# Six K and V loads of a two-layer decode kernel, each issued as 96 rows and four times 8 rows

## The chip, the cores and the metric

One core of one Trainium2 chip runs the whole kernel. The metric is the device time of one execution in microseconds (us), and the time before is the median of three runs. All operands are bf16 in device memory; the engines compute out of an on-chip memory of 128 partitions, and 16 DMA engines bring the data there.

## What is computed

Four sequences are at one new token each (B = 4, Sq = 1, D = 512). Block A is grouped-query attention over a cache: 32 query heads share 8 K and V heads, 4,096 cached positions, head width 128. Block B is a gated feed-forward of width F = 1,792. The two blocks are applied twice, with the same weights and the same caches:

```python
def _A_ref(x, k_cache, v_cache, wq, wo):
    q = (x @ wq).reshape(B, Sq, 32, 128).transpose(0, 2, 1, 3)
    k = jnp.repeat(k_cache, 4, axis=1)          # (4, 8, 4096, 128) -> 32 heads
    v = jnp.repeat(v_cache, 4, axis=1)
    scores = jnp.einsum("bhqd,bhkd->bhqk", q, k) * (128 ** -0.5)
    o = jnp.einsum("bhqk,bhkd->bhqd", softmax(scores), v)
    return o.transpose(0, 2, 1, 3).reshape(B, Sq, 4096) @ wo

def _B_ref(x, w_gate, w_up, w_down):
    return (sigmoid(x @ w_gate) * (x @ w_up)) @ w_down

x = x + _A_ref(_layernorm(x), ...)
x = x + _B_ref(_layernorm(x), ...)
x = x + _A_ref(_layernorm(x), ...)
x = x + _B_ref(_layernorm(x), ...)
```

One K head of one sequence is 4,096 x 128 bf16, that is 1 MB, and so is one V head. There are 32 of each.

## The kernel before

**Units.** A unit is one K head and one V head of one sequence in one layer: 2 x 4 x 8 = 64 units. `ORDER` lists them by hand in pairs, the second layer interleaved with the first as soon as a sequence has its input. For a pair the kernel transposes K (DVE, L1164), takes the scores (PE, L1180), reduces the maximum (DVE, PE L1199 and L1240), takes the exponential (ACT, L1265), turns the probabilities (PE L1310, ACT L1344) and multiplies them with V (PE, L1414). Query projection, the output projection with `wo`, the norms and block B stand between the units, at places that more tables at the head of the file fix by hand.

**Slots.** The on-chip memory has 12 slots of 128 partitions x 8 KB, each for one K or V head (`slot`); the four slices of `wq` become slots 12 to 15 once the queries of the second layer are done. A K head lies in its slot as `(p j) d -> p (j d)`: partition p holds 32 consecutive positions, 8 KB that are contiguous in device memory. V lies the same way, except that V of a pair with `SHARE` above 5 (`by_quarters`, L545) and the last two V come in quarters of 2 KB per partition (the last two V as four transfers each, `v_parts`, L517). `RET` says which heads stay in their slots from the first layer to the second and aren't loaded again.

**Loads.** The strings `LOADS` give the order in which everything is loaded: k, v, o (a piece of `wo`, L528) and s (a piece of the feed-forward weights, L528). The letters k and v count through the units in their order, so ("k", 9) is K of unit 9; units whose head is resident are skipped. `pump()` is called between the steps of the computation and issues, all on SP (SyncE), the next loads in this order as long as a slot is free in the plan; the transfer itself then waits on its semaphore until the last reader of that slot is done. SP issues nothing else but the first loads (L563, L566) and the output (L2084).

**Semaphores.** `_Sched` records all instructions by engine. `group` appends a list of instructions; the first of them gets the waits that follow from what is read and written, and the token of the last is what later readers wait for. `dma` is a group of one transfer that adds 16 to the semaphore of its slot when it has landed (`d0` to `d11`, `wq0` to `wq3`). `prune` and `assign_values` then drop waits that others imply and turn tokens into counts. So a reader of a slot waits until the slot's semaphore has reached a number.

Each load of a K or V head is one transfer of 128 rows, which the last statement of `pump()` issues (L550 in the profile).

Of the kernel before, what the change touches and what calls it, by code (L numbers as in the profile page):

```python
# [169 lines left out]
    71, 124, 3, 38, 71, 44, 6, 4,  # L170
    10,
)


class _Token:
# [135 lines left out]
def bass_interleave_layers__gqa_block_cached__glu_gated_glu__decode_kernel(  # L311
# [17 lines left out]
    P = 128  # L329
# [13 lines left out]
    NSLOT = 12  # L343
# [8 lines left out]
    S = _Sched()  # L352
# [144 lines left out]
    def slot_keys(s):  # L497
        return [f"s{s}"] + ([f"wq{s - NSLOT}"] if s >= NSLOT else [])

    def take():  # L500
        return free.pop(0)

    def by_quarters(n):
        return n < NU - 2 and SHARE[n // 2] > 5
# [5 lines left out]
    def v_parts(s, n):  # L510
        _, b, u = seq[n]
        rows = A_v_cache[b, u].rearrange("(a p j) d -> a p (j d)", a=4, p=P)
        for a in range(4):
            dst = slot[s][:, a * JG * DH:(a + 1) * JG * DH]
            S.dma(
                "sp",
                (lambda dst, src: lambda e: e.dma_start(dst, src))(dst, rows[a]),  # L517
                f"wo{4 * (n % 2) + a}",
                writes=[f"v{n % 2}_{a}"] + (slot_keys(s) if a == 0 else []),
            )  # L520

    def pump():
        while loads:
            kind, n = loads[-1]
            if kind in wparts:
                loads.pop()
                dst, src = wparts[kind](n)
                S.dma("sp", (lambda dst, src: lambda e: e.dma_start(dst, src))(dst, src), f"wo{n}" if kind == "wo" else kind, writes=[f"{kind}{n}"])  # L528
                continue
            if not free:  # L530
                return
            loads.pop()
            s = take()
            _, b, u = seq[n]
            if kind == "k":
                where["kn", n] = s
                src = A_k_cache[b, u].rearrange("(p j) d -> p (j d)", p=P)
            else:
                where["v", b, u] = s
                if n >= NU - 2:  # L540
                    v_parts(s, n)
                    continue
                src = A_v_cache[b, u].rearrange("(p j) d -> p (j d)", p=P)
            dst = slot[s][:, :]
            if kind == "v" and by_quarters(n):  # L545
                dst = dst.rearrange("p (a m) -> p a m", a=4)
                src = A_v_cache[b, u].rearrange("(a p j) d -> p a (j d)", a=4, p=P)
            S.dma(
                "sp",
                (lambda dst, src: lambda e: e.dma_start(dst, src))(dst, src),  # L550
                f"d{s}" if s < NSLOT else f"wq{s - NSLOT}",
                writes=slot_keys(s),
            )

# [6 lines left out]
    for k in range(KD):  # L561
        if k == 1:
# [5 lines left out]
            writes=[f"wq{k}"],  # L568
        )
    pump()  # L570

    dve(lambda e: e.memset(ones_f, 1.0), writes=["ones_f"])
# [18 lines left out]
    fns = []  # L591
# [882 lines left out]
    def o_turn(g):  # L1474
        p = g % 2
        many = 2 - PV_WIDE[g]
        s = stage.pop()
        o_raw = slot[s].bitcast(dt.float32)[:, 0:2 * P * many]
        act(lambda e: e.activation(o_raw, O_ps[p][:, 0:2 * P * many], ACTF.Copy), reads=[f"O{p}"], writes=slot_keys(s))
        fns = []  # L1480
        for n in range(2 * many):
            r = n * REP
            fns.append(
                (lambda n, r: lambda e: e.matmul(
                    O_ps[p][:, 0:2 * OW].rearrange("p (t w) -> p t w", t=2)[:, :, 0:REP],
                    lhsT=o_raw[:, n * P:(n + 1) * P],
                    rhs=o_sel[:, :, r:r + REP],
                    start=(n == 0),
                    stop=(n == 2 * many - 1),
                ))(n, r)  # L1490
            )
        S.group("pe", fns, reads=slot_keys(s) + ["o_sel"], writes=[f"O{p}"])
        free.append(s)
        pump()
# [113 lines left out]
    for m in wo_steps.pop((-1, 0), ()):  # L1608
        wo_turn(m, (M_ps, S_ps)[m % 2], "MS"[m % 2])
    k_turn(0)  # L1610
    pump()
    k_turn(1)
    pump()
# [17 lines left out]
    for b in range(Bn):  # L1631
        n = vstep[last[0, b]] - 1
# [499 lines left out]
```

## Time and profile before

| | |
|---|---|
| Runs | 303.77, 302.91, 303.86 us, median 303.77 |
| Span of the profiled execution | 306.1 us (no time of its own beside it; 0.8% above the median) |
| Granted TensorE clock, mean | 0.88 |
| Instructions | 11,460, of which PE 4,993, DVE 600, ACT 521, POOL 107 |
| Moved | 117.40 MB in 20,094 packets, 384 GB/s over the span |
| Last stretch without loads | from about 292 us to the end |

The profile's page gives first the busy time of each engine, then the span in 40 equal slices (7.65 us each) as tenths, then the DMA queues, the chain of work that ended last, the costliest groups of instructions, and the DMA issues with the median time from issue to landing. A row of the timeline or the chain begins with its start and its length in us. "SPq L550" is SP's issue of a load at line 550; "slot<-in_A_k_cache_dram" is the transfer of a K head into a slot. In a row of stretches the numbers in brackets are instruction counts, and behind them stand the granted clock, the DMA share and the rate in GB/s. In a row of waits the three numbers are the time waited in all, how often, and the longest.

### The profile page before, as it was taken

Reading aid. Unit: us, or ns where it says so; the run is one execution under the profiler, and the core shown is the slowest. Engines: PE = TensorE matmul, PEld = TensorE weight load, DVE = VectorE, ACT = ScalarE, POOL = GpSimd, SP = SyncE. Lnnn points to the kernel's source line nnn. Section 1 sums busy time; section 2 is a strip of 40 time slices with the busy share of each in tenths; the row PEclk is TensorE's granted clock in tenths of the full one; section 3 lists DMA queues with packets and bytes.
Section 4 is the critical chain, followed back from the end, with each engine's and each line's share of the span. In section 5 each row is a group of like instructions: output and inputs, shape, how many; then the busy total and the mean of one; then the engine's idle time right before and its main releaser. Section 6 shows DMA issues by size and latency. Waiting matters only on the chain.

```text
span 306.1 us, 11460 instructions
## 1 busy us (share of the span) xinstructions
PE 224.3 (73%) x4993; PEld 157.6 (51%) x4993; DVE 205.7 (67%) x600; ACT 131.2 (43%) x521; POOL 26.0 (9%) x107
## 2 busy tenths in 40 slices
PE   0384386864687888688886777888868688987886
PEld 0331043543464466566554554665546456556676
DVE  4755677885766368875854997566788668357743
ACT  1031243552205246564451874627772443646310
POOL 0000000000000010000001110001000000012200
PEclk9999999999579897979999857589788979599977
DMA  7999999999999979999999999999999999999900
GB/s 283 420 397 415 422 414 416 418 418 421 418 416 403 388 295 418 423 415 416 388 394 378 415 422 421 419 418 422 420 416 418 413 412 415 400 345 411 377 18 3
DMA packets 20094, 117.40 MB, mean 384 GB/s; under 512 B 1992, under 2 KB 1996, under 8 KB 7500
## 3 DMA queue, kind: packets, MB, share of 16 engines
q1 hardware_dynamic: 20044, 116.67, 93.9%
q8 instruction: 39, 0.64, 0.8%
q14 instruction: 11, 0.09, 0.1%
HBM read 116.66 MB, written 0.00 MB: 381 GB/s over the span
## 4 chain that ended last, share of the span: by engine, by line
DMA 45%; PE 30%; DVE 12%; SPq 5%; ACT 4%; issue 3%; POOL 0%; POOLq 0%; DVEq 0%; ACTq 0%
DMA slot<-in_A_v_cache_dram 22%; DMA slot<-in_A_k_cache_dram 12%; PE O_ps L1414 9%; DMA wd<-in_B_w_down_dram 6%; DVE slot L1164 6%; DMA wo<-in_A_wo_dram 5%; PE S_ps L1180 5%; ACT pT L1344 2%; SPq L550 2%; SPq L528 2%; PE M_ps L636 2%; PE O_ps L1566 2%; PE M_ps L1034 1%; PE M_ps L1087 1%; DVE wo L651 1%
## 5 line engine op out<-in xcount | busy, mean ns | idle before, releaser
L1164 DVE STREAM_TRANSPOSE slot<-slot 128x1024 f32<-128x1024 f32 (+1 forms) x61 | 100.9, 1663 | 7.0 <-DMA slot<-in_A_k_cache_dram 6.9
L1344 ACT ACTIVATE pT<-PT 32x64 bf16<-32x64 f32 x392 | 84.3, 215 | 31.9 <-PE PT L1310 26.9
L1414 PE MATMUL O_ps<-pT,slot 128*128 128x32 bf16 (+2 forms) x1888 | 65.8, 190 | 16.2 <-DMA slot<-in_A_v_cache_dram 9.6
L1414 PEld LDWEIGHTS O_ps<-pT,slot 128*128 128x128 bf16 x1888 | 59.6, 101 | 23.3 <-DMA slot<-in_A_v_cache_dram 10.6
L1180 PE MATMUL S_ps<-slot,qz 128*32 128x256 bf16 x1008 | 48.9, 329 | 12.5 <-DVE slot L1164 7.2
L1265 ACT ACTIVATE pe<-S_ps,small 128x256 bf16<-128x256 f32 x32 | 15.2, 474 | 63.3 <-DVE small L1253 63.2
L1180 PEld LDWEIGHTS S_ps<-slot,qz 128*32 128x32 bf16 x1008 | 25.3, 107 | 24.8 <-DVE slot L1164 9.2
L1279 POOL TENSOR_TENSOR small<-small 128x1 f32<-128x1 f32 x64 | 12.4, 193 | 217.6 <-ACT pe L1265 215.1
L646 ACT ACTIVATE wo<-M_ps 128x512 bf16<-128x512 f32 x14 | 8.3, 595 | 35.0 <-PE M_ps L636 35.0
L1338 DVE CAST pT<-PT 32x64 bf16<-32x64 f32 x88 | 19.4, 221 | 5.6 <-PE PT L1310 4.1
L1566 PE MATMUL O_ps<-oT,wo 128*128 128x32 bf16 x576 | 19.7, 188 | 1.1 <-issue 0.5
L636 PE MATMUL M_ps<-wo,row 64*128 64x512 bf16 x56 | 13.3, 565 | 9.1 <-DVE wo L651 5.5
L1566 PEld LDWEIGHTS O_ps<-oT,wo 128*128 128x128 bf16 x576 | 18.2, 101 | 2.1 <-DVE oT L1505 1.1
L1217 DVE TENSOR_REDUCE small<-S_ps 128x1 f32<-128x256 f32 x32 | 13.2, 413 | 8.0 <-PE S_ps L1180 7.8
L903 POOL TENSOR_TENSOR qz<-qc,norm 128x128 bf16<-128x128 bf16 x32 | 12.6, 399 | 45.5 <-ACT qc L889 45.5
L1240 PE MATMUL MS<-row_max,mask_f 128*128 128x16 bf16 x64 | 6.6, 176 | 13.1 <-DVE row_max L1223 12.6
L651 DVE CAST wo<-M_ps 128x512 bf16<-128x512 f32 x14 | 9.5, 680 | 9.6 <-PE M_ps L636 9.5
L1505 DVE TENSOR_TENSOR oT<-O_ps,rden 128x8 bf16<-128x8 f32 x31 | 4.9, 159 | 14.4 <-PE O_ps L1414 9.8
L1240 PEld LDWEIGHTS MS<-row_max,mask_f 128*128 128x128 bf16 x64 | 4.3, 107 | 19.2 <-DVE row_max L1223 17.7
L1199 PE MATMUL MS<-ident_bf 128*128 128x256 bf16 x69 | 12.2, 316 | 0.4
L1310 PE MATMUL PT<-ident_bf,pe 128*128 128x128 bf16 x64 | 10.0, 245 | 2.9 <-ACT pe L1265 2.6
L1253 DVE CUSTOM_DVE_ANT_0 row_max<-MS,small 128x16 bf16<-128x16 f32 x32 | 7.0, 217 | 7.3 <-PE MS L1240 7.1
(143 smaller groups left out, 231.1 us busy)
## 6 DMA issues: line engine op xcount, KB each, us to landing
slot<-in_A_v_cache_dram SPq DMA_DIRECT2D x49, 1024.0 KB, 12.5
slot<-in_A_k_cache_dram SPq DMA_DIRECT2D x43, 1024.0 KB, 11.3
wq<-in_A_wq_dram SPq DMA_DIRECT2D x4, 1024.0 KB, 7.8
wo<-in_A_wo_dram SPq DMA_DIRECT2D x8, 512.0 KB, 15.8
wq<-in_A_v_cache_dram SPq DMA_DIRECT2D x3, 1024.0 KB, 12.3
slot<-in_A_v_cache_dram SPq DMA_DIRECT2D x8, 256.0 KB, 13.6
wg<-in_B_w_gate_dram SPq DMA_DIRECT2D x2, 896.0 KB, 18.9
wu<-in_B_w_up_dram SPq DMA_DIRECT2D x2, 896.0 KB, 16.2
```

The lines of the kernel that those rows point to most:

```text
L636: (lambda h, i, rows: lambda e: e.matmul(ps[h][:, :], lhsT=spread_w[i][rows, :], rhs=wo_sb[rows, c + i, :], start=(i == 0), stop=(i == 1), ...
L651: lambda e: e.tensor_copy(wo_sb[:, c + 1, :], ps[1][:, :]),
L903: lambda e: e.tensor_tensor(qz_sb[z][:, :, 0:4 * REP].rearrange("p i (a r) -> p i a r", r=REP), qc_sb[:, b, u:u + 2, :, :].rearrange("p u ...
L1164: dve(lambda e: e.transpose(kf, kf), writes=[f"s{st}"])
L1180: (lambda t, b2, e_, w0, s: lambda e: e.matmul(S_ps[p][32 * s:32 * s + 8 * REP, 0:2 * P], lhsT=qzf[:, w0:w0 + 8 * REP], rhs=ktv[:, :, s, : ...
L1217: lambda e: e.tensor_reduce(m, S_ps[p][:, 0:2 * P], AX.X, ALU.max),
L1265: lambda e: e.activation(to, frm, ACTF.Exp, bias=nm_sb[p], scale=exp_scale, accum_out=sm_sb[p][0],),
L1279: (lambda n: lambda e: e.tensor_tensor(sm_sb[p][n + 1], sm_sb[p][n], top(sm_sb[p][n]), ALU.subtract))(n),
L1338: (lambda dst, frm: lambda e: e.tensor_copy(dst, frm))(dst, frm),
L1344: (lambda dst, frm: lambda e: e.activation(dst, frm, ACTF.Copy))(dst, frm),
L1414: (lambda x, c, j: lambda e: e.matmul(O_ps[p][:, ul * OW:ul * OW + PV_WIDE[g]].rearrange("p (w n) -> p w n", n=REP), lhsT=vv[:, x * JG + c ...
L1566: (lambda c, r: lambda e: e.matmul(wide_out(O_ps[p], OWO + c, nb), lhsT=wo_sb[:, u * REP + r, bass.ds(2 * P * (c // 2) + c % 2, P, step=2) ...
```

## The change

Two tables are new, and the last statement of `pump()` builds a group of one transfer per slice of partitions in place of one transfer:

```diff
+EIGHTS = (slice(0, 96), slice(96, 128, 4), slice(97, 128, 4), slice(98, 128, 4), slice(99, 128, 4))
+
+PARTS = {
+    ("k", 9): EIGHTS, ("k", 18): EIGHTS, ("v", 23): EIGHTS,
+    ("k", 40): EIGHTS, ("k", 49): EIGHTS, ("v", 52): EIGHTS,
+}
...
-            S.dma(
+            fns = []
+            for rows in PARTS.get((kind, n), (slice(0, P),)):
+                fns.append((lambda dst, src: lambda e: e.dma_start(dst, src))(dst[rows], src[rows]))
+            S.group(
                 "sp",
-                (lambda dst, src: lambda e: e.dma_start(dst, src))(dst, src),
-                f"d{s}" if s < NSLOT else f"wq{s - NSLOT}",
+                fns,
+                sem_key=f"d{s}" if s < NSLOT else f"wq{s - NSLOT}",
+                inc=16,
+                needed=True,
                 writes=slot_keys(s),
             )
```

For six of the loads the first transfer has the partitions 0 to 95 and each of the four others has eight of the partitions 96 to 127, four apart: 96, 100, ..., 124, then 97, 101, ..., 125, and so on. Each of the five adds 16 to the slot's semaphore, 80 in all, and a reader of the slot waits for all of them. All other loads, their order, and the instructions of all other engines are as before. The lines below the tables move down by 8, and L550 becomes L558.

The six loads go, in the profiled execution before, to slot 5 (issued near 45.6 us), slot 12 (108.3 us), slot 9 (143.0 us), slot 12 (183.1 us), slot 5 (219.3 us) and slot 2 (251.5 us).

## The prediction on record

> **What bounds the kernel now.** I read the page from the top: the DMA lines first, then the chain, then the stretches of time.
>
> ```profile
> span 306.1 us, 11460 instructions
> ...
> DMA  7999999999999979999999999999999999999900
> GB/s 283 420 397 415 422 414 416 418 418 421 418 416 403 388 295 418 423 415 416 388 394 378 415 422 421 419 418 422 420 416 418 413 412 415 400 345 411 377 18 3
> DMA packets 20094, 117.40 MB, mean 384 GB/s; under 512 B 1992, under 2 KB 1996, under 8 KB 7500
> ...
> q1 hardware_dynamic: 20044, 116.67, 93.9%
> q8 instruction: 39, 0.64, 0.8%
> q14 instruction: 11, 0.09, 0.1%
> ...
> DMA 45%; PE 30%; DVE 12%; SPq 5%; ACT 4%; issue 3%; POOL 0%; POOLq 0%; DVEq 0%; ACTq 0%
> ```
>
> The 16 DMA engines are busy for nine tenths or more in all but two of the first 38 slices, and 45% of the chain that ended last is DMA. So this is a kernel that streams, with short places where the stream breaks. Those places are seen in the stretches (columns: window, its length, five engines' busy time, granted clock, DMA share, GB/s):
>
> ```profile
> 60.00:104.00 44.00, 31.20 (x630) 21.63 (x626) 28.77 (x81) 15.05 (x58) 2.25 (x10) 0.84 1.01 414
> 104.00:112.00 8.00, 6.56 (x166) 4.06 (x167) 4.99 (x22) 2.58 (x10) 0.76 (x2) 1.00 0.80 297
> ...
> 120.00:147.00 27.00, 21.61 (x485) 16.15 (x482) 18.77 (x48) 14.61 (x66) 2.21 (x9) 0.90 1.01 418
> 147.00:156.00 9.00, 7.35 (x189) 5.42 (x186) 6.32 (x26) 5.12 (x19) 0.48 (x3) 1.00 0.99 373
> ...
> 176.00:248.00 72.00, 55.95 (x1322) 41.03 (x1318) 52.42 (x139) 38.99 (x165) 6.95 (x29) 0.78 1.01 418
> ...
> 268.00:277.00 9.00, 7.69 (x206) 5.53 (x206) 5.45 (x23) 4.64 (x20) 1.49 (x5) 0.94 0.99 353
> ```
>
> Three long stretches run at 414 to 418 GB/s with every engine full. At 104 to 112, 147 to 156 and 268 to 277 us the rate falls to 297, 373 and 353: there some engines have nothing queued. The chain, in order of time (start, length, piece), says which loads the end hangs on:
>
> ```profile
> 60.33 14.42 DMA slot<-in_A_k_cache_dram
> ...
> 79.90 18.77 DMA wd<-in_B_w_down_dram
> ...
> 112.88 11.82 DMA slot<-in_A_v_cache_dram
> ...
> 125.92 13.82 DMA slot<-in_A_v_cache_dram
> ...
> 142.97 6.67 DMA slot<-in_A_v_cache_dram
> ...
> 207.72 10.57 DMA slot<-in_A_v_cache_dram
> ...
> 219.34 13.83 DMA slot<-in_A_k_cache_dram
> ...
> 239.34 8.69 DMA slot<-in_A_k_cache_dram
> 248.05 1.85 DVE slot L1164
> ```
>
> The last transfer on it lands at 239.34 + 8.69 = 248.03 us. After that the chain is compute and issue alone, down to the end.
>
> **What one load is.** Issues by kind (count, size, median us from issue to landing):
>
> ```profile
> slot<-in_A_v_cache_dram SPq DMA_DIRECT2D x49, 1024.0 KB, 12.5
> slot<-in_A_k_cache_dram SPq DMA_DIRECT2D x43, 1024.0 KB, 11.3
> wq<-in_A_wq_dram SPq DMA_DIRECT2D x4, 1024.0 KB, 7.8
> ...
> wq<-in_A_v_cache_dram SPq DMA_DIRECT2D x3, 1024.0 KB, 12.3
> ...
> wq<-in_A_k_cache_dram SPq DMA_DIRECT2D x1, 1024.0 KB, 7.8
> ```
>
> Packets of 8 KB or more: 20,094 − 7,500 = 12,594. The 1 MB loads of K, V and wq are 49 + 43 + 4 + 3 + 1 = 100; two V loads go by quarters (2 KB pieces), and 98 × 128 rows = 12,544, plus the 50 packets of the two instruction queues, is 12,594 exactly. So a row is one packet. One costs its engine 0.939 × 16 × 306.1 us / 116.67 MB × 8,192 B = 0.323 us. A whole load is 8 packets per engine, 2.58 us; the stream's 418 GB/s gives 2.5. Landing comes 11 to 12.5 us after issue, so four to five loads stand in the queues.
>
> **The change, part by part.** It moves the same bytes in the same rows: packets stay 20,094 and no engine besides SP gets an instruction more. SP gets six times four more issues. The six loads in its issue order (start, us, count in the row):
>
> ```profile
> 44.65 1.36 SPq L550 DMA_DIRECT2D slot<-in_A_k_cache_dram  x2
> ...
> 108.25 4.16 SPq L550 DMA_DIRECT2D slot<-in_A_k_cache_dram  x4
> ...
> 142.97 8.91 SPq L550 DMA_DIRECT2D slot<-in_A_v_cache_dram  x5
> ...
> 183.07 0.33 SPq L550 DMA_DIRECT2D slot<-in_A_k_cache_dram  x1
> ...
> 219.34 0.33 SPq L550 DMA_DIRECT2D slot<-in_A_k_cache_dram  x1
> ...
> 248.88 14.02 SPq L550 DMA_DIRECT2D slot<-in_A_v_cache_dram  x6
> ```
>
> They are the second of the first row, the first of the second and third, the fourth and fifth, and the second of the sixth. Two of them, at 142.97 and 219.34, are themselves pieces of the chain.
>
> *Issues on SP.* One costs 0.33 us, four 1.3 us per split. Nothing new waits: only the 96-row transfer carries the slot's wait. Queued behind it on SP are the next loads, and behind those, compute. What hides it is that SP itself waits for slots most of the time:
>
> ```profile
> SPq L550 <- PE O_ps L1414: 69.0, 26, 4.4
> SPq L550 <- PE S_ps L1180: 55.4, 25, 5.8
> ```
>
> Alone these two are 124 us. With 10 us of transfers queued, 1.3 us more on SP starves nothing, except perhaps at 108.25, where engines are dry and three loads wait behind: 0 to 1.3 us there. I take 0, since the 96 rows give every engine 1.9 us of work before the next load is needed. Without that cover all six would cost 7.8 us.
>
> *Completion.* Readers now wait for five transfers. The last is issued 1.3 us after the first and queues for some 10 us; I cost this at nothing, up to 0.3 us in the load that took only 6.67 us.
>
> *Work per engine.* This is the term that counts. The 96 rows are 6 packets on each engine if they are dealt as evenly as the 128. A transfer of 8 rows is 8 packets, so half the engines get none of it. No row of before shows a transfer of that shape. Bounds: if four such transfers are dealt in turn over all 16 engines, each engine has 8 packets as before, cost 0. If all four go to the same eight, those have 6 + 4 = 10 (3.23 us) and the others 6 (1.94 us), that is 0.65 us above and 0.65 us below the whole load. I take the second end: transfers of one shape, issued one after the other, have no visible reason to be dealt differently. A load has landed when its slowest engine is done, and in a full stream the slow eight stay 0.65 us behind until the queues run dry. So a split costs 0.65 us if the engines were even before.
>
> The sum by stage. The load at 45 us is ahead of the transfers at 60.33 and 79.90, in the stretch at full rate: 0.65. That at 108.25 comes at the end of the first break, ahead of 112.88 and 125.92, and the one at 142.97 is itself on the chain: 1.3. Those of 183.07 and 219.34 lie in the third full stretch, ahead of 207.72, 219.34 and 239.34: 1.3. The sixth, after 248.88, has no transfer of the chain behind it and a break at 268 to absorb it: 0; if the later loads became bound, 0.65. In sum 5 × 0.65 = 3.2 us. I make it against the profiled execution (span 306.1 us) and add it to the median of the runs, 303.77; the profiled one is 0.8% longer, which changes 3.2 by 0.03. Forecast: **307.0 us**.
>
> [...]
>
> **The rivals.**
>
> *Faster: the engines are uneven now, and the change evens them.* The instruction queue's 39 fetches take 0.8% × 16 × 306.1 = 39 us, 1.0 us each. If they all land on the same eight engines, these lose 4.9 us each over the run, the others nothing, and the stream goes at the pace of the eight. If the eight that the small transfers spare are exactly those, six splits give them 6 × 1.29 = 7.7 us relative to the others, against 4.9: the lag is taken away, and then somewhat overdone. The gain is half the lag that builds up in a stretch without a break: 4.9/306 = 0.016 us per us, in stretches of about 44, 35 and 72 us 0.7 + 0.56 + 1.15 = 2.4, half 1.2 us: 302.6. If a fetch costs its engine half as much again, 302.0. For it: any unevenness is invisible in a share of 1.01 averaged over 16 engines. Against it: no grouped row says where the fetches land, and if they fall on the eight that get more, the forecast grows by the same 1.2 us. It decides as soon as the fetched-on eight lag by more than 0.65 us when a split comes.
>
> *Much slower: the two eights get in each other's way at the memory.* The small transfers write partitions 96 to 127. [...] If two engines that share a way into those partitions run at half pace for four packets, that is 1.29 us more on each; the heavy eight then need 3.23 + 1.29 = 4.52 us instead of 2.58, 1.94 us more per split, five of them 9.7 us: 313.5. At half that overlap, 308.6. For it: 418 GB/s is the flat top of the rate line, so something is full; against it: nothing in the rows says whether it is the engines or the way into memory.
>
> [...]
>
> *Nothing: the small transfers are dealt over all engines, or the queues absorb the lag.* 303.8 us. For it: DMA is only 45% of the chain.
>
> **How the numbers follow.** Forecast case (0.9 to 5 us slower) 0.36; much slower 0.20; faster 0.32; nothing 0.12. A measurement of this kernel can tell about 0.3%, 0.9 us. Of the faster case 0.27 is beyond that and 0.05 within; of the last case 0.02 on either side. So faster 0.29, same 0.13, slower 0.58. Range 302.0 to 312.0: from the faster case with the dearer fetch to the much slower one nearly whole, leaving out some 0.08 below and 0.09 above.
>
> **What would show it.** Right: loads issued behind a split land later by about 0.65 us; the chain's pieces at 60.33, 112.88, 207.72 and 239.34 grow; the rate in the full stretches falls from 418 for some us behind each split and the breaks are filled by the light eight. The fast rival: those pieces shrink, and the full stretches hold their rate while the breaks get deeper and earlier. The much slower one: the rate falls clearly in slices with a split, below 400. The issue term is wrong if SP's waits for slots shrink and DMA share falls right behind a split. The forecast is wrong if the even deal before the change, on which 0.65 rests, isn't so.

## The result and the profile after

The changed kernel takes 331.72 us (median of four runs, 329.24 to 336.21), the kernel before beside it 303.81. The ratio is 1.089, 95% interval 1.082 to 1.097. Ratios here and below leave out the few runs that fell into a slower state of the chip, such as the one of 336.21 us. By the ratio that is 27 us more, 4.5 us for each of the six loads, over eight times the rise that was forecast, and above the range's upper end of 312.0. The execution profiled after has a span of 331.4 us.

The page of the changed kernel, the lines that answer to those of before:

```profile
span 331.4 us, 11484 instructions
...
DMA  7999999999999599999989999999999999999930
GB/s 296 416 404 416 422 410 418 280 341 418 421 404 411 196 287 418 419 420 317 265 306 381 414 423 358 276 421 420 420 346 229 402 389 388 254 419 395 407 136 4
DMA packets 20286, 117.40 MB, mean 354 GB/s; under 512 B 2184, under 2 KB 2188, under 8 KB 7692
...
q1 hardware_dynamic: 20236, 116.67, 94.2%
...
DMA 44%; PE 32%; DVE 10%; SPq 6%; issue 3%; ACT 3%; POOL 1%; POOLq 0%; DVEq 0%; ACTq 0%
```

Read the second and third line together. The rate falls to 280, 287, 265, 276, 229 and 254 GB/s in slices 8, 15, 20, 26, 31 and 35, one for each split, and in all six the DMA engines are shown nine tenths busy. So they are not starved: their packets take longer, 0.557 us in the stretch below where the mean of before is 0.323. The slice with 196 GB/s is another case: its digit is 5, and it is the break that the kernel before has too. Share times span of q1 gives the time that an engine spends on packets: 0.939 × 306.1 = 287.4 us before, 0.942 × 331.4 = 312.2 us after, for the same 116.67 MB. That is 24.8 us more per engine, against 25.3 us more span. The loss is nearly all time in which packets are under way.

The stretches around the splits, first the kernel before and then the changed one (window, length, five engines' busy time, granted clock, DMA share, GB/s):

```profile
60.00:70.00 10.00, 6.44 (x160) 4.28 (x153) 8.88 (x21) 5.93 (x24) 0.74 (x3) 1.00 1.01 420
```

```profile
60.00:70.00 10.00, 6.26 (x110) 3.94 (x111) 6.40 (x18) 4.19 (x16) 0.31 (x2) 0.59 1.02 240
70.00:104.00 34.00, 23.81 (x451) 16.32 (x448) 21.60 (x58) 9.63 (x39) 1.54 (x7) 0.70 1.02 414
...
152.00:164.00 12.00, 5.10 (x84) 3.22 (x84) 6.95 (x21) 2.01 (x7) 0.39 (x2) 0.72 1.02 264
...
274.00:286.00 12.00, 8.19 (x180) 5.71 (x179) 8.43 (x24) 4.93 (x18) 0.39 (x2) 0.90 1.03 323
```

From 60 to 70 us, when the first split load passes through the engines, all of them are busy (1.02) and they move 240 GB/s in place of 420. An 8 KB packet then takes 1.02 × 16 × 10 us / 2.4 MB × 8,192 B = 0.557 us, where 0.323 is the mean of before. Right behind it, from 70 us, the rate is back at 414. This loses (420 − 240)/420 × 10 = 4.3 us at one split. The 2.4 MB that pass in these 10 us are as much as 18 packets of 8 KB per engine, and the split load has 8 of them, if its rows are shared out evenly. So packets of the loads around it are slow as well.

Who waits for it stands in the rows of waits of the changed kernel (time in all, times, longest):

```profile
PE O_ps L1427 <- DMA slot<-in_A_v_cache_dram: 23.4, 14, 5.7
...
DVE slot L1177 <- DMA slot<-in_A_k_cache_dram: 19.3, 11, 6.4
```

and in those of the kernel before:

```profile
PE O_ps L1414 <- DMA slot<-in_A_v_cache_dram: 9.6, 12, 1.9
...
DVE slot L1164 <- DMA slot<-in_A_k_cache_dram: 6.9, 7, 1.9
```

PE waits 13.8 us longer for V and DVE 12.4 us longer for K, 26.2 us together (the two can overlap). The chain of the changed kernel has the pieces that the forecast named, longer:

```profile
59.63 19.57 DMA slot<-in_A_k_cache_dram
...
237.98 0.66 SPq L558
238.68 0.62 SPq L558
239.34 0.62 SPq L558
240.01 17.44 DMA slot<-in_A_k_cache_dram
...
272.96 11.25 DMA slot<-in_A_v_cache_dram
```

The K load of 60.33 took 14.42 us before and takes 19.57 now. The piece at 240.01 is the last small transfer of the fifth split, with three issues of that split ahead of it on the chain; the whole load, at 219.34 before, took 13.83 us. The last piece is new: a V load issued ahead of the sixth split now ends a wait after 248 us.

### The profile page after: what moved, and what is told of

The parts are those of the page before. It is cut to its first block, busy times and chain, and to the rows that moved or that the text cites. A ratio compares the mean times of both kernels' runs of the same rounds, so it can differ in the third digit from the quotient of the medians.

```text
span 331.4 us, 11484 instructions
## 1 busy us (share of the span) xinstructions
PE 230.9 (70%) x4993; PEld 161.8 (49%) x4993; DVE 206.6 (62%) x600; ACT 130.9 (39%) x521; POOL 26.0 (8%) x107
## 2 busy tenths in 40 slices
DMA packets 20286, 117.40 MB, mean 354 GB/s; under 512 B 2184, under 2 KB 2188, under 8 KB 7692
## 3 DMA queue, kind: packets, MB, share of 16 engines
q1 hardware_dynamic: 20236, 116.67, 94.2%
## 4 chain that ended last, share of the span: by engine, by line
DMA 44%; PE 32%; DVE 10%; SPq 6%; issue 3%; ACT 3%; POOL 1%; POOLq 0%; DVEq 0%; ACTq 0%
DMA slot<-in_A_v_cache_dram 23%; DMA slot<-in_A_k_cache_dram 11%; PE O_ps L1427 10%; DMA wd<-in_B_w_down_dram 6%; PE S_ps L1193 5%; DVE slot L1177 5%; DMA wo<-in_A_wo_dram 5%; SPq L558 3%; PE M_ps L1047 3%; PE O_ps L1579 2%; SPq L536 2%; ACT pT L1357 1%; PE M_ps L649 1%; PE M_ps L1100 1%; DVE pT L1351 1%
## 5 line engine op out<-in xcount | busy, mean ns | idle before, releaser
L1427 PE MATMUL O_ps<-pT,slot 128*128 128x32 bf16 (+2 forms) x1888 | 68.9, 194 | 29.2 <-DMA slot<-in_A_v_cache_dram 23.4
L1427 PEld LDWEIGHTS O_ps<-pT,slot 128*128 128x128 bf16 x1888 | 62.9, 103 | 35.9 <-DMA slot<-in_A_v_cache_dram 22.6
L1193 PE MATMUL S_ps<-slot,qz 128*32 128x256 bf16 x1008 | 50.6, 340 | 17.3 <-DVE slot L1177 9.2
L1292 POOL TENSOR_TENSOR small<-small 128x1 f32<-128x1 f32 x64 | 12.4, 193 | 244.4 <-ACT pe L1278 241.9
L1518 DVE TENSOR_TENSOR oT<-O_ps,rden 128x8 bf16<-128x8 f32 x31 | 5.0, 160 | 24.8 <-PE O_ps L1427 21.5
L1253 PE MATMUL MS<-row_max,mask_f 128*128 128x16 bf16 x64 | 6.6, 176 | 13.8 <-DVE row_max L1236 13.0
L1047 PE MATMUL M_ps<-wq,xc_bf 128*1 128x512 bf16 x128 | 11.6, 463 | 0.7 <-DVE xc_bf L778 0.5
## 6 DMA issues: line engine op xcount, KB each, us to landing
slot<-in_A_v_cache_dram SPq DMA_DIRECT2D x47, 1024.0 KB, 13.8
```

Of the source, the lines that this page charges most:

```text
L1047: (lambda k, st: lambda e: e.matmul(M_ps[h][32 * st:32 * st + 1, :], lhsT=xc_bf[:, k, 0:1], rhs=wv[:, k, h, :, st, :], start=(k == 0), sto ...
L1193: (lambda t, b2, e_, w0, s: lambda e: e.matmul(S_ps[p][32 * s:32 * s + 8 * REP, 0:2 * P], lhsT=qzf[:, w0:w0 + 8 * REP], rhs=ktv[:, :, s, : ...
L1427: (lambda x, c, j: lambda e: e.matmul(O_ps[p][:, ul * OW:ul * OW + PV_WIDE[g]].rearrange("p (w n) -> p w n", n=REP), lhsT=vv[:, x * JG + c ...
```

## The experiments

Theory P, a guess from the slow packets above (0.557 us where 0.323 was the mean): engines that write at the same time into the same partitions slow each other, so packets take twice as long. The rivals are N, the number of transfers and their issue; U, the uneven share of rows per engine, which was the forecast's term; S, that any transfer below 128 rows is slow; and R, that the place is where rows are read. All experiments change only the tuple `EIGHTS` for the same six loads, except where said. Ratios are to the kernel before on the same chip, with 95% intervals.

**1. Five transfers of 128 rows each.**

```diff
-EIGHTS = (slice(0, 96), slice(96, 128, 4), slice(97, 128, 4), slice(98, 128, 4), slice(99, 128, 4))
+EIGHTS = tuple((slice(0, 128), slice(a, b)) for a, b in ((0, 1024), (1024, 2048), (2048, 3072), (3072, 3584), (3584, 4096)))
```

> Same six loads, each as five transfers on one semaphore, but every transfer has all 128 rows and a part of the columns (three of 2 KB a row, two of 1 KB). Theory P (engines that write into the same partitions halve each other's pace): no change to the partitions, so within 1.5 us of 303.8. Rival N (the number of transfers or their issue costs, 28 us for 24 more): 320 to 332. Rival U (only the uneven share of the engines, as forecast): 303.8.

Measured: 307.80 us, 1.011 (1.003 to 1.018). As many transfers on the same semaphore as in the change cost 3 us, not 27. N falls as the main cause. The 3 us are above what P expected. Part of them is seen on the chain, where the issues of two splits stand for 1.4 us each (144.19 to 145.62 and 218.75 to 220.17 us); experiment 14 returns to the rest.

**2. 96 rows and 32 rows.**

```diff
+EIGHTS = (slice(0, 96), slice(96, 128))
```

> Each of the six loads as 96 rows and one transfer of 32 rows (two per engine). P: the 96 rows and the 32 rows are both slowed, about 1.9 and 0.6 us per split: 314 to 320. N: a quarter of the transfers added, a quarter of the loss: 311. U: every engine has 8 rows again: 303.8.

Measured: 327.23 us, 1.075 (1.067 to 1.082). Here each engine has 6 + 2 = 8 rows again, if they are dealt evenly, and one transfer is added in place of four. More than four fifths of the loss remain, 23 of 27 us. U and N both fall; the value is above the 314 to 320 that I had given P, whose sizes I had underestimated.

**3. The 96 rows alone.**

```diff
+EIGHTS = (slice(0, 96),)
```

> Leaves out rows 96 to 127 of the six loads (stale data there), so 1.5 MB less is moved, worth 3.9 us by the packets. P: the 96 rows alone take nearly twice their 1.9 us: 306 to 311. N and U: nothing is split and the engines are even, so 300.

Measured: 321.47 us, 1.058 (1.053 to 1.063). The kernel moves 1.5 MB less and takes 17.6 us longer, 2.9 us for each of the six. So a loss of this size, two thirds of the whole, needs no small transfer at all: the transfer of 96 rows brings it. P had the sign, but under half the size.

**4. The small transfers alone.**

```diff
+EIGHTS = (slice(96, 128, 4), slice(97, 128, 4), slice(98, 128, 4), slice(99, 128, 4))
```

> Leaves out rows 0 to 95 of the six loads and keeps the four transfers of 8 rows, so 4.5 MB less is moved, worth 11.6 us. P: half the engines spend four rows at half pace or worse and slow the other half meanwhile, 2.5 to 3.5 us in place of 2.58 for a whole load: 303 to 309. N: four transfers cost most of the 4.7 us per split: 310 to 320. U: 1.3 us in place of 2.58 on the busier engines: 296 to 298.

Measured: 309.68 us, 1.021 (1.014 to 1.027). A quarter of the data of these loads takes 6.3 us longer than all of it. So the small transfers cost something as well. Parts 3 and 4 are not to be added: each leaves data out, and how much of its packets' worth that saves is not measured.

**5. The split turned over.**

```diff
+EIGHTS = (slice(32, 128), slice(0, 32, 4), slice(1, 32, 4), slice(2, 32, 4), slice(3, 32, 4))
```

> The same split turned over: rows 32 to 127 in one transfer, rows 0 to 31 in four of eight rows, four apart. [...] If only the second half of the memory were slow for the small transfers, or if the number of transfers counted, 328 to 332 or as the change. [...]

Measured: 327.22 us, 1.074 (1.067 to 1.081). The small transfers now write partitions 0 to 31. Most of the loss remains, 23 of 27 us, so it does not hang on the upper partitions.

**6. Two halves of 64 rows.**

```diff
+EIGHTS = (slice(0, 64), slice(64, 128))
```

> Each of the six loads as two transfers of 64 rows, 0 to 63 and 64 to 127. Same count of transfers as 96 and 32 rows, every engine again has 8 rows. [...] A theory S, by which a transfer of fewer than 128 rows is slow whatever its rows: as 96 and 32 rows, 327. U: 304.

Measured: 330.23 us, 1.087 (1.081 to 1.093). One transfer more per load, none of it small, and every engine even if the rows are dealt evenly: it costs as much as the whole change. This fits S. Whether it fits P hangs on which engines write which partitions, and no row shows that.

**7 and 8. Four transfers of 32 rows: every fourth row, and neighbouring rows.** These two differ in nothing but the rows that each transfer takes.

```diff
+EIGHTS = tuple(slice(i, 128, 4) for i in range(4))
```

> Each of the six loads as four transfers of 32 rows, every fourth row from 0, 1, 2 and 3, so that each transfer reaches all parts of the memory. [...] S: as the four transfers of neighbouring rows. U: 304.

```diff
+EIGHTS = tuple(slice(32 * i, 32 * i + 32) for i in range(4))
```

> Each of the six loads as four transfers of 32 neighbouring rows. [...] S: the same as with every fourth row. U: 304.

Measured: 307.86 us, 1.012 (1.004 to 1.019), with every fourth row; 331.59 us, 1.092 (1.083 to 1.100), with neighbouring rows. S falls: the same size and number of transfers costs 4 us or 28. Page and stretch of the strided kernel:

```profile
span 304.1 us, 11478 instructions
...
DMA packets 20382, 117.40 MB, mean 386 GB/s; under 512 B 2280, under 2 KB 2284, under 8 KB 7788
...
q1 hardware_dynamic: 20332, 116.67, 94.3%
```

```profile
60.00:70.00 10.00, 6.72 (x144) 4.87 (x145) 8.56 (x20) 4.56 (x18) 0.74 (x3) 0.83 1.02 420
```

and of the one with neighbouring rows:

```profile
span 328.1 us, 11478 instructions
...
q1 hardware_dynamic: 20332, 116.67, 94.9%
```

```profile
60.00:70.00 10.00, 4.43 (x86) 2.81 (x87) 6.07 (x17) 3.58 (x14) 0.00 (x0) 0.80 1.02 251
```

With every fourth row an engine spends 0.943 × 304.1 = 286.8 us on packets, as in the kernel before (287.4); with neighbouring rows 0.949 × 328.1 = 311.4. At 60 to 70 us the rates are 420 and 251 GB/s, at the same DMA share of 1.02.

The count of packets under 512 B goes with the rows of the transfers. It rises from 1,992 to 2,184 with the change, by 8 for each of its 24 small transfers, and the 96 rows leave the count of their load as it was (1,992 in experiment 3); with 18 added transfers of 32 rows it rises to 2,280, by 16 each. Read as one small packet from each engine that has a part of the transfer, this would be 8 engines for 8 rows and 16 for 32; that reading is my estimate from the counts, and which engines they are no row shows.

**9 and 10. Reading and writing taken apart.** `PARTS` gives a pair here, the partitions written and the rows read:

```diff
-            for rows in PARTS.get((kind, n), (slice(0, P),)):
-                fns.append((lambda dst, src: lambda e: e.dma_start(dst, src))(dst[rows], src[rows]))
+            for to, of in PARTS.get((kind, n), ((slice(0, P), slice(0, P)),)):
+                fns.append((lambda dst, src: lambda e: e.dma_start(dst, src))(dst[to], src[of]))
```

```diff
+EIGHTS = tuple((slice(i, 128, 4), slice(32 * i, 32 * i + 32)) for i in range(4))    # 9
+EIGHTS = tuple((slice(32 * i, 32 * i + 32), slice(i, 128, 4)) for i in range(4))    # 10
```

> Each of the six loads as four transfers of 32 rows that are read from neighbouring rows of the cache and written to every fourth partition. This changes the computation: the rows of these six heads lie in other partitions than their counterparts. If the loss comes from where the rows are written (P): as the four strided transfers, 306 to 309. If it comes from where they are read (R): as the four neighbouring ones, 330.

> The counterpart: read from every fourth row of the cache, written to 32 neighbouring partitions; the rows of these six heads again lie elsewhere. P: 329 to 333. R: 306 to 309.

Measured: written to every fourth partition 307.99 us, 1.014 (1.010 to 1.019); written to neighbouring ones 331.44 us, 1.091 (1.087 to 1.094). The time follows the partitions written and not the rows of the cache that are read. The stretch of the two kernels, 9 and then 10:

```profile
60.00:70.00 10.00, 7.74 (x139) 5.12 (x143) 8.42 (x19) 4.40 (x18) 0.74 (x3) 0.55 1.01 419
```

```profile
60.00:70.00 10.00, 4.82 (x74) 2.51 (x75) 5.85 (x14) 3.61 (x14) 0.00 (x0) 0.58 1.03 196
```

R falls: what counts is the partitions that a transfer writes. That is the part of P that the two pairs show; that engines slow each other there is its reading, which fits the times, and no row shows the single engines. P's factor of two is too small here: at 196 GB/s an 8 KB packet takes 1.03 × 16 × 10 us / 1.96 MB × 8,192 B = 0.689 us, over twice 0.323. The clock column also rules out a cause that the page of the changed kernel might suggest, its lower granted clock (0.59 in this stretch): kernel 9 has 0.55 there and keeps its 419 GB/s.

**11. The idea of the change without its 96 rows.**

```diff
+EIGHTS = tuple(slice(i, 128, 4) for i in range(3)) + tuple(slice(i, i + 29, 4) for i in (3, 35, 67, 99))
```

> The change's idea without its 96 rows: three transfers of 32 rows, every fourth row, then the last 32 rows as four transfers of eight, so that half the engines again have four rows more than the others. If sparing the other half is worth something (the rival that I priced at 1.2 to 1.8 us): 304 to 307, below the four strided transfers. [...] U, the forecast's own term of 0.65 us: 310 to 311.

Measured: 316.36 us, 1.039 (1.035 to 1.044). Three quarters are written as in experiment 7, where all four quarters cost 1.2%, and the last 32 rows go in transfers of eight rows each. That is 8.5 us above the strided split, 1.4 us per load, where U had 0.65. If the small transfers all go to the same eight engines, which no row shows, sparing the others earns nothing that outweighs this. Whether the instruction fetches burden one half of the engines is not settled by it.

**12. Only the sixth split.**

```diff
-PARTS = {("k", 9): EIGHTS, ..., ("v", 52): EIGHTS}
+PARTS = {("v", 52): EIGHTS}
```

> Only the last of the six splits, issued near 251 us. My forecast costed it at 0 because no transfer is on the chain after 248 us: 303.8. If the late loads become the bound as soon as the stream loses 4 us: 306 to 309.

Measured: 307.05 us, 1.012 (1.009 to 1.014), 3.5 us for the one split that I had costed at nothing. The chain of this kernel:

```profile
236.19 8.54 DMA slot<-in_A_v_cache_dram
...
248.15 12.07 DMA slot<-in_A_v_cache_dram
```

The V load issued just ahead of the split stands on the chain for 12.07 us and lands at 260.2, and PE waits 2.9 us for it. The same load, issued at 248.88, took 9.1 us in the kernel before. So even a load issued earlier than the split one is slowed with it. I read this as engines that are ahead and already write the split load's rows while others still bring the earlier load; no row shows the single engines.

**13. Even and odd rows.**

```diff
+EIGHTS = (slice(0, 128, 2), slice(1, 128, 2))
```

> Each of the six loads as two transfers of 64 rows, the even and the odd ones: the same counts as the halves, which took 330.2, but every transfer reaches all parts of the memory. P, with no cost of the number of transfers: 303.8. P, with a cost of 0.2 us for each added transfer (from the strided 32 rows): 304.5 to 305.5. S, any transfer below 128 rows: 330.

Measured: 305.41 us, 1.006 (1.002 to 1.010), against 1.087 for the two halves. A second pair with equal counts, and the same answer.

**14. Twelve loads in strided quarters.**

```diff
+EIGHTS = tuple(slice(i, 128, 4) for i in range(4))
+PARTS = {(kind, n): EIGHTS for kind in "kv" for n in (9, 18, 23, 40, 49, 52)}
```

> Twelve loads, K and V of units 9, 18, 23, 40, 49 and 52, as four transfers of every fourth row. If the 1.2% of the six strided ones is a cost of each added transfer (about 0.2 us): 311 to 313. If it belongs to single places or to the spread between runs: 306 to 309.

Measured: 307.91 us, 1.011 (1.008 to 1.014). With 6, 18, 18, 24 and 36 added transfers (13, 7, 9, 1 and 14) the ratios are 1.006, 1.012, 1.014, 1.011 and 1.011. That is not a price per transfer. Apart from the issues on the chain in experiment 1, what these 2 to 4 us are stays open.

**What P does not give** is the size. Per split load the change costs 4.5 us (0.089 × 303.8 / 6), the halves 4.4, the neighbouring quarters 4.6 and the strided ones 0.6. P's figures were too low in experiments 2 and 3. How the rows of a transfer below 128 are dealt to the engines, and so which engines write beside which, no row shows, and it stays open.

## Why the prediction was wrong, point by point

- **What bounds the kernel, what one load is:** held in the main. The stream is the bound, and a row is one packet. The packets of 8 KB or more are 20,286 − 7,692 = 12,594 as before. "Packets stay 20,094" was wrong by the 192 small ones.
- **The breaks:** "there some engines have nothing queued" fits only the first, with its share of 0.80. At 147 to 156 and 268 to 277 us the share is 0.99, 2% below the 1.01 of the full stretches, while the rate is 11% and 16% below 418. So nearly all engines were at work there and moved less, and the rows of before already showed, with none of these splits, a nearly full share beside a lower rate. What slows the loads there no experiment tests.
- **Issues on SP, cost 0:** too low. The five issues of the fifth split take 0.62 us in the median, not 0.33, and three of them stand on the chain, 2.03 us from 237.98 to 240.01. But this is the smaller part: as many more issues in experiment 1 cost 3 us in all, and experiment 2, with a quarter of them, keeps 23 of 27.
- **Completion, cost 0:** no run shows a cost of its own. In experiment 1 readers also wait for five transfers on one semaphore.
- **Work per engine, the term that counts, 0.65 us per split:** this is the step that failed. It asked how many packets an engine gets, and took it that the 96 rows are "6 packets on each engine if they are dealt as evenly as the 128" and that each packet keeps its 0.323 us. Experiment 2 makes the counts even again, if the rows are dealt evenly, and keeps 23 of 27 us; experiment 3 has no small transfer and keeps 17.6. What counts in its place is which partitions each transfer writes: where the split writes neighbouring ones, a packet takes 0.557 us in the first split's stretch. Experiments 7 to 10 show it with sizes and counts equal. That the four transfers of eight rows go to the same eight engines, from which the 10 and 6 packets and the 0.65 us follow, no run shows; what the runs show of it is eight more packets under 512 B for each of these transfers.
- **The much slower rival:** nearest to what the runs show, with a chance of 0.20 and the wrong place and price. Its sign, a rate below 400 in the slices with a split, came in all six. It had only the small transfers collide, "half pace for four packets", 1.94 us per split and 313.5 us. It left the 96 rows at full pace, and these alone bring 17.6 us. No run shows that two engines share a way into partitions 96 to 127, or that they run at half pace there; what the runs show is that the time follows the partitions written, 1.014 against 1.091 in experiments 9 and 10.
- **The sum by stage:** "The sixth, after 248.88 ... 0" was wrong. Alone it costs 3.5 us (experiment 12). That no transfer stood on the chain after 248 us did not mean that the loads there had time to spare: in the kernel before, PE's weight load already waited 0.2 us for the V load issued at 248.88.
- **The faster rival:** no support. In experiment 11, which takes the 96 rows away and keeps the transfers of eight rows, the time is 12 us above the kernel before.
- **The bounds:** 0 and 0.65 us per split were bounds on the packet count only. The case that every packet of a split runs at half pace was left out. It gives 2.58 us per split and 15.5 for six, 319, and even that is short of the 4.5 us measured, because packets of other loads are slowed too.

## What to carry to other kernels

Before a transfer is cut by partitions, ask which partitions each piece writes, not only how many packets each engine gets: six loads in pieces of every fourth or every second partition cost 1.2% and 0.6% here, in pieces of neighbouring partitions 8.7% to 9.2%, with equal sizes and counts. In a profile the sign was a DMA share of 1.02 or 1.03 beside 196 to 264 GB/s. A full share beside a low rate says that packets take longer (0.557 us here where 0.323 was the mean), and not yet why. If a load in a stretch like these must be divided, try its columns first, which cost 1.1% here, or its partitions with a stride.

## What the runs showed of the hardware that I had not expected

- The same 32-row transfers, reordered in the partitions that they write, changed the rate in one stretch from 419 to 196 GB/s (experiments 9 and 10).
- Transfers of 96 rows in place of 128 in six loads make the kernel 5.8% slower, though each moves a quarter less (experiment 3).
- The slow-down covers the neighbours too: in the changed kernel 2.4 MB pass in 10 us at 240 GB/s, and 1 MB of that is the split load.
